# Keeping PSUM copies back to set places, and moving fill transfers to other queues, in a top-k attention and mixture-of-experts kernel

## The chip, the core and the metric

The kernel runs on one core of one Trainium2 chip. A core has TensorE (PE, matmuls; its weight loads are shown as PEld), VectorE (DVE), ScalarE (ACT), GpSimd (POOL) and SyncE (SP). They run side by side, each takes its instructions in the order of its own queue, and semaphores hold an instruction until what it needs is done. Matmuls write to PSUM, and another engine copies the result to SBUF, the working memory. DMA transfers are issued from SyncE's, ScalarE's or GpSimd's queue; 16 DMA engines carry them. The metric is the device time of one execution in microseconds; lower is better.

## The reference

Attention with the 32 largest scores per row, then a mixture of eight experts in which each token goes to the one expert with the largest gate value:

```python
batch, n_heads, seq, head_dim = (8, 8, 576, 64)
scores = scale * np.matmul(q, k.transpose(0, 1, 3, 2))
kth = np.partition(scores, -top_k, axis=-1)[..., -top_k:-top_k + 1]   # top_k = 32
scores = np.where(scores >= kth, scores, -1e9)
attn = softmax(scores); attn_out = np.matmul(attn, v)
x = attn_out.transpose(0, 2, 1, 3).reshape(4608, 512)                 # tokens
logits = x @ w_gate                                                    # 8 experts
e = argmax(logits); gate_w = softmax(logits)[e]
y = gate_w * (np.maximum(x @ w1[e], 0) @ w2[e])      # w1 512x1024, w2 1024x512
```

All of it is in 32-bit floats.

## The kernel before

**Attention.** The work is cut into 160 steps: 8 batches, 4 units of two heads, 5 groups of query tiles (four groups of two tiles of 128 rows, and one group of a single tile). For a step, TensorE forms the scores (`sc`, L244), ScalarE copies them to SBUF (`s`, L253), VectorE folds each row to half its length (`h` and `l`, L260, L262) and finds the threshold of the 32 largest by repeated MAX8 and MATCH_REPLACE8 (L302 to L327). GpSimd scales the threshold (`low`, L329), ScalarE applies it (`depths`, L341), GpSimd subtracts (`less`, L350), ScalarE takes the exponential (`weights`, L361). One step later TensorE transposes the weights (`wTm`, L375, and the rest of the row, `wTl`, L384), ScalarE copies them (`wT`, `wTt`), and at the end of a unit TensorE multiplies with the values (`po`, L405). Scores are formed three steps ahead.

**Routing.** At the end of a batch each token gets its expert and its row in `x_rows`, a buffer in DRAM in which each expert has a stretch of its own. GpSimd scatters the tokens there (L517). After the last batch each expert's last, partly filled block of 128 rows is filled up with blank rows: `fill_up` (L532) waits for all scatters, reads where each expert ends (`value_load`) and issues one transfer of 128 blank rows for each of the eight experts (L539), and one more (L543). In the kernel before, the odd experts' fills are on ScalarE's queue and the even ones' on SyncE's.

**The MoE blocks.** 40 blocks of 128 rows are computed. For each, SyncE loads the rows (`xg`, L612) and the weights of its expert (`w1` and `w2`, 2048 KB each, L604 and L606; two buffers of each, and two of `xg`, whose buffer comes free when the block's result has been stored). `turned` (L622) transposes the rows on TensorE (`xtp`) and copies them out of PSUM (`xTs`, L628). `block` (L630) then does the first layer in two halves of four pieces (`ph`, four matmuls to a piece, L641), each half followed by the ReLU into `hT` on ScalarE (L646), then `py` in eight pieces of one matmul (L650), and the scaled copy `y` (L653). GpSimd stores the rows of `y` (L656). Ahead of `py`, `following` puts out waiting stores and transposes the rows of the next block. `block` is a generator, and each `yield` ends a piece; a block has 16.

**The order.** TensorE, VectorE and ScalarE get their instructions in exactly the order in which the program writes them (`manual_schedule`). `loop` (L850 on) writes one attention step after another, and twice in each step `pieces(n)` runs some pieces of the current block: once between the `wTm` and `wTl` transposes, and once at the end. A rate per batch says how many. So a piece's copies stand on ScalarE at the place where `pieces` happened to reach them. In batches 3 to 8 the loop computes some 24 blocks; two blocks are kept to be run at its end, while the last tokens are routed, and the 14 last ones follow. Four PSUM tiles of MoE work (`xtp`, `ph` twice, `py`) go through two buffers.

The generator's core in the kernel before:

```python
            nc.scalar.activation(hT[:, half * (FT // 2):(half + 1) * (FT // 2), :], ph, AF.Relu)
        following()
        py = k.ps_m.tile([P, Dm], F32, name="py", tag="m")
        for f in range(FT):
            nc.tensor.matmul(py, hT[:, f, :], n.w2[:, 0, f, :], start=(f == 0), stop=(f == FT - 1))
            yield "last" if f == FT - 1 else None
        y = k.mlp.tile([P, Dm], F32, name="y")
        nc.scalar.activation(y, py, AF.Copy, scale=n.x[:, 0, Dm:Dm + 1])
```

Of the kernel before, what the change touches and what calls it, by code (L numbers as in the profile page):

```python
# [11 lines left out]
AF = mybir.ActivationFunctionType  # L12
# [31 lines left out]
def kernel(  # L44
# [487 lines left out]
    def fill_up():  # L532

        ends = k.small.tile([1, E], I32, name="ends")
        nc.vector.tensor_copy(ends, run[0:1, :])
        for e in range(E):
            on = nc.scalar if e % 2 else nc.sync
            r = on.value_load(ends[0:1, e:e + 1], min_val=e * CAP, max_val=e * CAP + N)
            put = on.dma_start(x_rows[bass.ds(r, P), :], blank).ins  # L539
            if not k.exact:  # L540
                for other in scattered:
                    tc.add_manual_dep(put, other.name, WAIT)
        nc.sync.dma_start(x_rows[EMPTY * P:(EMPTY + 1) * P, :], blank)  # L543
# [78 lines left out]
    def turned(n):  # L622

        ps = k.ps_m.tile([P, DT, P], F32, name="xtp", tag="m")
        for dt in range(DT):
            nc.tensor.transpose(ps[:, dt, :], n.x[:, 0, dt * P:(dt + 1) * P], ident)
        n.xT = k.mlp.tile([P, DT, P], F32, name="xTs")
        nc.scalar.copy(n.xT, ps)  # L628

    def block(n, following=lambda: None, put_off=lambda store: store()):  # L630

        if not hasattr(n, "xT"):
            turned(n)
            yield
        hT = k.mlp.tile([P, FT, P], F32, name="hT")
        for half in range(2):
            ph = k.ps_m.tile([P, FT // 2, P], F32, name="ph", tag="m")
            for f in range(FT // 2):
                fc = half * (FT // 2) + f
                for dt in range(DT):  # L640
                    nc.tensor.matmul(  # L641
                        ph[:, f, :], n.w1[:, 0, dt, fc * P:(fc + 1) * P], n.xT[:, dt, :],
                        start=(dt == 0), stop=(dt == DT - 1),
                    )
                yield
            nc.scalar.activation(hT[:, half * (FT // 2):(half + 1) * (FT // 2), :], ph, AF.Relu)  # L646
        following()
        py = k.ps_m.tile([P, Dm], F32, name="py", tag="m")
        for f in range(FT):
            nc.tensor.matmul(py, hT[:, f, :], n.w2[:, 0, f, :], start=(f == 0), stop=(f == FT - 1))  # L650
            yield "last" if f == FT - 1 else None
        y = k.mlp.tile([P, Dm], F32, name="y")
        nc.scalar.activation(y, py, AF.Copy, scale=n.x[:, 0, Dm:Dm + 1])  # L653

        def store():
            put = nc.gpsimd.indirect_dma_start(  # L656
                out=out[:, :], out_offset=bass.IndirectOffsetOnAxis(ap=n.x[:, 0, Dm + 1:XW].bitcast(I32), axis=0),
                in_=y[:, :], in_offset=None, bounds_check=N - 1, oob_is_err=False,
            )
            if not k.exact:  # L660
                tc.add_manual_dep(put.ins, k.last_pool.name, AFTER)

        put_off(store)

    PIECES = 2 * FT
    FIRST = 13
# [5 lines left out]
    with ExitStack() as st:  # L672
# [7 lines left out]
        per_batch = U * len(groups)  # L680
        x_of, lg_of = {}, {}
        waiting, loaded, coming, spare, scatters, stores = [], [], [], [], [], []
        current = ended = None
        left = clock = 0

        def landed(n):
# [5 lines left out]
                loaded[-1].at = clock  # L692

        def put_stores():
            nonlocal current, ended
            while stores:
                stores.pop(0)()
            if ended == "last":
                ended = next(current, "end")
                current = None  # L700

        def following():
            put_stores()
# [1 line left out]
                turned(loaded[0])  # L705

        def pieces(n):
            nonlocal current, left, ended
            if ended == "last":
                ended = next(current, "end")  # L710
                current = None
            while n > 0 and left > 0:
                if current is None:
                    if not landed(loaded[0]):
                        break
                    now = loaded.pop(0)
                    if not hasattr(now, "xT"):
                        turned(now)
                    current = block(now, following, stores.append)
                    ahead()  # L720
                ended = next(current, "end")
                if ended == "end":
                    current = None
                else:
                    n -= 1
                    left -= 1
            return n

        def scatter(n):
# [107 lines left out]
        def loop():  # L837
            nonlocal credit, rate, clock
            for i in range(min(AHEAD, len(work))):
                multiply(i)  # L840
                s_of[i], steps = scores(got_of.pop(i))
                for step in steps:
                    step()
            multiply(AHEAD)
            hl_of[0] = fold(work[0][2], s_of[0])
            for i, (b, u, g) in enumerate(work):
                n = unit[b * U + u]
                if g == groups[0]:
                    open_unit(n)

                if i + 1 < len(work):
                    hl_of[i + 1] = fold(work[i + 1][2], s_of[i + 1])
                low, nbias = search(n, g, s_of[i], *hl_of.pop(i))
                at_place("small")
                w_of[i] = depths(g, s_of[i], low)
                less(g, s_of.pop(i), w_of[i])
                put_stores()
                scatter(1)
                at_place("pool")
                at_place("relu")  # L860
                at = i % per_batch
                if at == FIRST and b:
                    rate = new_of[b - 1] * PIECES / (U * NT)
                credit += rate * len(g)
                room = left
                if b == B - 1 and at >= ARRIVED:
                    room -= KEEP
                    credit = room * len(g) / sum(len(x[2]) for x in work[i:])
                share = 0.5 if g in (groups[0], groups[-2]) else 1.6 if g == groups[2] else 1.2 if g == groups[1] else 1
                now = max(0, min(int(credit * share + 0.5), room))  # L870
                credit -= now
                clock = i
                if i + AHEAD < len(work):
                    s_of[i + AHEAD], steps = scores(got_of.pop(i + AHEAD))
                    for step in steps:
                        step()
                at_place("turn")
                if i:
                    turns = turning(i - 1)
                    next(turns)  # L880
                rest = pieces(now - now // 2)
                if i:
                    next(turns, None)
                weights(n, g, w_of[i], nbias)
                if i + AHEAD + 1 < len(work):
                    multiply(i + AHEAD + 1)
                if g == groups[-2]:
                    end = ending(b, u)
                    late.append([end, next(end)])
                at_place("products")  # L890
                at_place("weights")
                credit = min(credit + pieces(now // 2 + rest), 6 * rate)

            for _ in turning(len(work) - 1):
                pass
            assert len(late) == 1
            clock = None
            for count, _ in enumerate(late[0][0]):
                if count == 4:
                    pieces(6)  # L900
            kept = left - ALWAYS * PIECES
            assert kept == KEEP - 6, kept
            pieces(kept)
# [2 lines left out]
        with tc.manual_schedule(engines={mybir.EngineType.PE, mybir.EngineType.Activation, mybir.EngineType.DVE}):  # L906
            loop()
        pieces(ALWAYS * PIECES)
        put_stores()
        put_stores()  # L910

        any_p = k.small.tile([P, 1], F32, name="any_p")
# [10 lines left out]
    with ExitStack() as outer:  # L923
        either = nc.values_load(rare_i[0:1, 0:1], min_val=0, max_val=P + 1)  # L924
        outer.enter_context(tc.If(either > 0))
        with ExitStack() as st:
            open_pools(st, True)
            more = nc.values_load(rest_i[0:1, 0:1], min_val=0, max_val=LAST)
            with tc.If(more > ALWAYS):
                for slot in spare:  # L930
                    for _ in block(load_block(*slot)):
                        pass
        again = nc.values_load(any_i[0:1, 0:1], min_val=0, max_val=P)
        outer.enter_context(tc.If(again > 0))
        with ExitStack() as st:
# [47 lines left out]
            with tc.For_i(0, NSLOT, 1) as j:  # L983
                now = keep.tile([1, 2], I32, name="now")
                for n in range(2):
                    nc.sync.dma_start(now[:, n:n + 1], slot_d[bass.ds(j + n * NSLOT, 1), :])
                for _ in block(load_block(now[0:1, 0:1], now[0:1, 1:2])):
                    pass


_OUTS = [((4608, 512), 'float32')]
# [40 lines left out]
```

## Time and profile before

| | |
|---|---|
| median of 3 runs | 1626.84 us (1624.94 to 1628.05) |
| profiled execution | 1625.93 us, span 1624.2 us |
| busy: PE, DVE, ACT, POOL | 1348.2, 1263.5, 913.1, 755.1 us |
| granted TensorE clock, mean | 0.906 of full speed |
| moved by DMA | 230.69 MB, 142 GB/s over the span |

The profile is of one execution. Times in it are microseconds from the span's start. Busy time is the time in which an engine executes; a wait is idle time of an engine ahead of an instruction, and it is put down to what ended it (`<-`). "SPq" and "ACTq" are queue entries, such as the issue of a DMA. A line number such as L646 is that of the kernel before; `out<-in` are tile names. "issue" as a releaser means that the engine's own queue was held by instructions that do not count as busy, such as register loads and their waits.

### The profile page before, as it was taken

To read this page: it belongs to the slowest core of one execution; us is meant where nothing else is said; L and a number is where in the kernel's file an instruction comes from. 1 tells how busy PE (TensorE), PEld (TensorE's weight loads), DVE (VectorE), ACT (ScalarE), POOL (GpSimd) and SP (SyncE) were. 2 spreads that over 40 slices of the span, in tenths; PEclk is the share of its full clock that TensorE was granted. 3 is DMA by queue.
4 is the path that set the end of the run, shared out by engine and by line. 5 is a ranking of instruction groups with operands and counts; after the bars stand their busy time and mean duration, and the time that the engine had idled before them with its cause. 6 is when DMAs were issued, how large, how long until landed. Compare 5 with 4: busy or idle time off the path is not lost. (4 is left out here: it accounts for less than half of the span.)

```text
span 1624.2 us, 25229 instructions
## 1 busy us (share of the span) xinstructions
PE 1348.2 (83%) x8034; PEld 891.9 (55%) x8034; DVE 1263.5 (78%) x4130; ACT 913.1 (56%) x1937; POOL 755.1 (46%) x993
## 2 busy tenths in 40 slices
PE   4776677667698989888989988989989995899996
PEld 2443344334465656555656655656656563576764
DVE  7999999999999999999899999999989930000000
ACT  4666666665676667666666766676656640111111
POOL 3555555555555565556544755564546531000000
PEclk9777887886799999999999999999989997899998
DMA  2000011001613343335444443434344638488883
GB/s 60 24 24 23 23 37 40 23 24 36 237 62 143 140 171 136 143 139 170 158 148 180 160 179 140 147 136 167 140 146 154 227 125 291 176 311 307 305 296 132
DMA packets 102191, 230.69 MB, mean 142 GB/s; under 512 B 5150, under 2 KB 25630, under 8 KB 102048
## 3 DMA queue, kind: packets, MB, share of 16 engines
q1 hardware_dynamic: 95328, 209.00, 36.1%
q0 software_dynamic: 6144, 18.92, 3.2%
q8 instruction: 66, 1.08, 0.3%
q10 hardware_dynamic: 576, 1.05, 0.2%
q14 instruction: 77, 0.63, 0.1%
HBM read 207.68 MB, written 22.33 MB: 142 GB/s over the span
## 5 line engine op out<-in xcount | busy, mean ns | idle before, releaser
L350 POOL TENSOR_TENSOR w<-s,w 128x576 f32<-128x576 f32 x288 | 400.3, 1409 | 311.7 <-ACT w L341 311.7
L302 DVE MAX8 tops<-scr 128x8 f32<-128x288 f32 x864 | 361.0, 447 | 3.1
L650 PE MATMUL py<-w,hT 128*128 128x512 f32 x640 | 315.7, 633 | 42.3 <-ACT hT L646 42.3
L641 PE MATMUL ph<-xTs,w 128*128 128x128 f32 x2560 | 322.4, 280 | 25.1 <-ACT xTs L628 25.1
L641 PEld LDWEIGHTS ph<-xTs,w 128*128 128x128 f32 x2560 | 304.5, 194 | 56.3 <-issue 29.8
L341 ACT ACTIVATE w<-s,low 128x576 f32<-128x576 f32 x288 | 209.7, 772 | 101.7 <-POOL low L329 101.3
L244 PE MATMUL sc<-qkb 64*128 64x288 f32 (+1 forms) x1280 | 239.9, 499 | 28.9 <-ACT s L253 23.1
L312 DVE MATCH_REPLACE8 scr<-tops,scr 128x288 f32<-128x288 f32 x576 | 251.0, 441 | 0.0
L361 ACT ACTIVATE w<-w,nbias 128x576 f32<-128x576 f32 x288 | 221.4, 772 | 0.4 <-POOL w L350 0.4
L650 PEld LDWEIGHTS py<-w,hT 128*128 128x128 f32 x640 | 120.0, 201 | 164.4 <-issue 116.3
L329 POOL TENSOR_SCALAR low<-thr 128x2 f32<-128x2 f32 (+1 forms) x160 | 86.3, 540 | 253.1 <-DVE thr L327 246.4
L375 PE MATMUL wTm<-ident,w 128*128 128x128 f32 x1152 | 175.7, 294 | 9.7 <-ACT x L423 8.1
L244 PEld LDWEIGHTS sc<-qkb 64*128 64x128 f32 (+1 forms) x1280 | 123.7, 207 | 97.4 <-ACT s L253 32.3
L375 PEld LDWEIGHTS wTm<-ident,w 128*128 128x128 f32 x1152 | 139.4, 150 | 68.0 <-issue 31.4
L384 PE MATMUL wTl<-ident,w 128*64 128x128 f32 x288 | 66.0, 306 | 131.9 <-ACT wT L378 131.3
L253 ACT COPY s<-sc 128x576 f32<-128x576 f32 x288 | 168.9, 634 | 9.5 <-PE sc L244 9.5
L405 PE MATMUL po<-wT,vb 128*64 128x288 f32 x1024 | 159.8, 461 | 0.6 <-ACT wT L380 0.6
L656 POOL DMA_INDIRECT out_dram<-y,xg x40 | 41.6, 1041 | 251.6 <-ACT y L653 247.8
L378 ACT COPY wT<-wTm 128x512 f32<-128x512 f32 x256 | 139.0, 604 | 3.1 <-PE wTm L375 3.1
L260 DVE TENSOR_TENSOR h<-s 128x576 f32<-128x576 f32 (+1 forms) x160 | 121.0, 756 | 25.0 <-ACT s L253 25.0
L312 DVE MATCH_REPLACE8 scr<-tops,h 128x288 f32<-128x288 f32 x288 | 125.4, 442 | 0.0
L384 PEld LDWEIGHTS wTl<-ident,w 128*64 128x64 f32 x288 | 28.1, 119 | 175.1 <-ACT wT L378 155.1
(124 smaller groups left out, 1491.4 us busy)
## 6 DMA issues: line engine op xcount, KB each, us to landing
w<-in_moe_w_dram SPq DMA_DIRECT2D x80, 2048.0 KB, 12.2
qkb<-in_qk_dram SPq DMA_DIRECT2D x32, 576.0 KB, 3.9
xg<-x_rows SPq DMA_DIRECT2D x40, 257.0 KB, 2.7
vb<-in_v_dram SPq DMA_DIRECT2D x32, 320.0 KB, 3.2
x_rows<-blank SPq DMA_DIRECT2D x5, 257.0 KB, 10.3
x_rows<-blank ACTq DMA_DIRECT2D x4, 257.0 KB, 7.9
x_rows<-x,posi POOLq DMA_INDIRECT x40, 3.1
out_dram<-y,xg POOLq DMA_INDIRECT x40, 2.8
```

Source lines behind the costliest of these rows:

```text
L244: nc.tensor.matmul(ps[rows, j, 0:HF], n.q[d, cols], n.k[d, j * HF:(j + 1) * HF], start=True, stop=True)
L253: lambda m=m, ps=ps: nc.scalar.copy(s[:, m, :, :], ps[:, :, 0:HF]) for m, ps in enumerate(got)
L302: nc.vector.max(out=tops[:, m, r * 8:(r + 1) * 8], in_=src[m])
L312: nc.vector.match_replace(out=scr[:, m, :], in_to_replace=tops[:, m, r * 8:(r + 1) * 8], in_values=src[m], imm_value=NEG,)
L341: nc.scalar.activation(w[:, m, :], s[:, m, :, :].rearrange("p j k -> p (j k)"), AF.Relu, scale=-STEEP, bias=low[:, m:m + 1],)
L350: k.last_pool = in_turn(nc.gpsimd.tensor_tensor(w[:, m, :], s[:, m, :, :].rearrange("p j k -> p (j k)"), w[:, m, :], op=ALU.subtract)).ins
L361: nc.scalar.activation(w[:, m, :], w[:, m, :], AF.Exp, scale=scale, bias=nbias[:, m:m + 1], accum_out=n.z[:, c + m:c + m + 1],)
L375: nc.tensor.transpose(pm[:, c * P:(c + 1) * P], w[:, m, c * P:(c + 1) * P], ident)
L378: nc.scalar.copy(n.wT[:, :, m, tiles[0] * P:(tiles[0] + 1) * P], pm4)
L405: nc.tensor.matmul(po[r, 0:HF], lhsT, rhs, start=(c == 0), stop=(c == KC - 1))
L641: nc.tensor.matmul(ph[:, f, :], n.w1[:, 0, dt, fc * P:(fc + 1) * P], n.xT[:, dt, :], start=(dt == 0), stop=(dt == DT - 1),)
L650: nc.tensor.matmul(py, hT[:, f, :], n.w2[:, 0, f, :], start=(f == 0), stop=(f == FT - 1))
```

## The change

Copies out of PSUM of the MoE blocks are no longer written where `pieces` reaches them. `turned`, the two halves of `block` and its end put them on a list, `due`, and `evacuate` writes out what is on the list, in order. In the loop this is done at two places in each step: behind `depths`, and behind `weights`. Inside `block` it is also done where a PSUM buffer or a result is needed next. After the transposes of the first block, and after the second half of every block, `block` yields "pause": in the loop `pieces` then stops, and goes on at the next of its places, by which time `evacuate` has written the copies. At the end of the program, where `clock` is None, nothing stops at a pause. The copy `y` and its store are put on the list in the same way. The fills of the odd experts go from ScalarE's queue to GpSimd's. The numbers of matmuls, copies and transfers are the same as before.

Where the first block starts, TensorE's rows before (`xtp`: transposed rows of the block, `ph`: its first layer, `wTl`: rest of the weights' transpose, `sc`: next scores, `po`: product with the values):

```order
L375 MATMUL wTm<-ident,w 128x128 x8
L626 MATMUL xtp<-ident,xg 128x128 x4
L641 MATMUL ph<-xTs,w_3831 128x128 x4
L384 MATMUL wTl<-ident,w 64x128 x2
L244 MATMUL sc<-qkb 128x288 x4
L405 MATMUL po<-wT,vb 64x288 x8
```

and now:

```order
L626 MATMUL xtp<-ident,xg 128x128 x4
L384 MATMUL wTl<-ident,w 64x128 x2
L244 MATMUL sc<-qkb 128x288 x4
L405 MATMUL po<-wT,vb 64x288 x8
L405 MATMUL po<-wTt,vb 64x288 x2
L651 MATMUL ph<-xTs,w_3831 128x128 x8
```

The first piece of `ph`, which stood ahead of `wTl`, `sc` and `po`, now stands behind them together with the next.

Late in the loop, ScalarE's rows before (`xTs` and `hT`: the copies of `xtp` and `ph`):

```order
L361 ACTIVATE w,z<-w,nbias 128x576 x2
L407 COPY oT_99<-po 128x288
L646 ACTIVATE hT<-ph 128x512
L628 COPY xTs<-xtp 128x512
L341 ACTIVATE w<-s,low 128x576 x2
L253 COPY s<-sc 128x576
```

and now:

```order
L361 ACTIVATE w,z<-w,nbias 128x576 x2
L656 ACTIVATE hT<-ph 128x512
L407 COPY oT_99<-po 128x288
L341 ACTIVATE w<-s,low 128x576 x2
L628 COPY xTs<-xtp 128x512
L253 COPY s<-sc 128x576
```

`hT` goes directly behind the exponentials, and `xTs` behind the depths (L341); the copy of the scores `s` stays behind `xTs`.

Where the loop ends, the kernel before has on SyncE, behind the load of `w1` for the block after the two kept ones:

```order
L604 DMA w_13697<-in_moe_w_dram 128x4x1024
L538 TENSOR_LOAD ends
L538 ISA x2
L539 ISA
L539 DMA x_rows<-blank 128x514
...
L606 ISA
L606 DMA w_13699<-in_moe_w_dram 128x8x512
...
L543 DMA x_rows<-blank 128x514
```

and on ScalarE:

```order
L784 COPY run<-rank 128x8
L538 TENSOR_LOAD ends
L538 ISA x2
L539 ISA
L539 DMA x_rows<-blank 128x514
...
L646 ACTIVATE hT<-ph 128x512
L628 COPY xTs<-xtp 128x512
```

Of ScalarE's four fills only the first is shown; on SyncE two stand ahead of `w2`, and two and the last one (L543) behind it. Now SyncE has the load of `w2` ahead of all its fills:

```order
L604 DMA w_13697<-in_moe_w_dram 128x4x1024
L606 ISA
L606 DMA w_13699<-in_moe_w_dram 128x8x512
L538 TENSOR_LOAD ends
L538 ISA x2
L539 ISA
L539 DMA x_rows<-blank 128x514
```

and on ScalarE `hT` follows the copy of `run` directly:

```order
L804 COPY run<-rank 128x8
L656 ACTIVATE hT<-ph 128x512
L628 COPY xTs<-xtp 128x512
L680 ACTIVATE y<-py,xg 128x512
L656 ACTIVATE hT<-ph 128x512 x2
```

On GpSimd the four fills stand behind the last five scatters and ahead of the next store of `y`. VectorE's rows are the same in both kernels; GpSimd's and SyncE's differ at this place alone.

The diff, cut to its core:

```diff
@@ fill_up
-            on = nc.scalar if e % 2 else nc.sync
+            on = nc.gpsimd if e % 2 else nc.sync
@@ turned
-        nc.scalar.copy(n.xT, ps)
+        due.append(("xT", lambda: nc.scalar.copy(n.xT, ps)))
+
+    due = []
+
+    def evacuate(upto=None):
+
+        while due and (upto is None or upto in [kind for kind, _ in due]):
+            due.pop(0)[1]()
 
     def block(n, following=lambda: None, put_off=lambda store: store()):
 
         if not hasattr(n, "xT"):
             turned(n)
-            yield
+            yield "pause"
+        evacuate()
         hT = k.mlp.tile([P, FT, P], F32, name="hT")
         for half in range(2):
+            if half:
+                evacuate("y")
             ph = k.ps_m.tile([P, FT // 2, P], F32, name="ph", tag="m")
...
+                if f == FT // 2 - 1:
+                    due.append((f"h{half}", lambda ph=ph, half=half: nc.scalar.activation(
+                        hT[:, half * (FT // 2):(half + 1) * (FT // 2), :], ph, AF.Relu
+                    )))
                 yield
-            nc.scalar.activation(hT[:, half * (FT // 2):(half + 1) * (FT // 2), :], ph, AF.Relu)
+        evacuate("h0")
         following()
+        yield "pause"
+        evacuate()
         py = k.ps_m.tile([P, Dm], F32, name="py", tag="m")
         for f in range(FT):
             nc.tensor.matmul(py, hT[:, f, :], n.w2[:, 0, f, :], start=(f == 0), stop=(f == FT - 1))
-            yield "last" if f == FT - 1 else None
+            if f < FT - 1:
+                yield
         y = k.mlp.tile([P, Dm], F32, name="y")
-        nc.scalar.activation(y, py, AF.Copy, scale=n.x[:, 0, Dm:Dm + 1])
...
+        def scaled():
+            nc.scalar.activation(y, py, AF.Copy, scale=n.x[:, 0, Dm:Dm + 1])
+            put_off(store)
+
+        due.append(("y", scaled))
+        yield "last"
@@ pieces
-                ended = next(current, "end")
-                if ended == "end":
+                if clock is None:
+                    evacuate()
+                step = next(current)
+                if step == "pause":
+                    if clock is not None:
+                        break
+                    continue
+                if step == "last":
                     current = None
-                else:
-                    n -= 1
-                    left -= 1
+                n -= 1
+                left -= 1
@@ loop
                 w_of[i] = depths(g, s_of[i], low)
+                evacuate()
                 less(g, s_of.pop(i), w_of[i])
                 put_stores()
...
                 weights(n, g, w_of[i], nbias)
+                evacuate()
```

More of the change, by code (lines that the diff above doesn't have):

```diff
@@ L661, in store, with whole_block @@
                 tc.add_manual_dep(put.ins, k.last_pool.name, AFTER)
-        put_off(store)
+        def scaled():
[3 more added lines that the diff above has]
+        yield "last"
+    def whole_block(n):
+        for _ in block(n):
+            evacuate()
     PIECES = 2 * FT
@@ L682 @@
         waiting, loaded, coming, spare, scatters, stores = [], [], [], [], [], []
-        current = ended = None
+        current = None
         left = clock = 0
@@ L694, in put_stores @@
         def put_stores():
-            nonlocal current, ended
             while stores:
                 stores.pop(0)()
-            if ended == "last":
-                ended = next(current, "end")
-                current = None
         def following():
@@ L707, in pieces @@
         def pieces(n):
[L708 to L711, printed above, removed]
+            nonlocal current, left
             while n > 0 and left > 0:
@@ L715, in pieces @@
                         break
[L716 to L719, printed above, removed]
+                    current = block(loaded.pop(0), following, stores.append)
                     ahead()
-                ended = next(current, "end")
-                if ended == "end":
+                if clock is None:
[6 more added lines that the diff above has]
+                if step == "last":
                     current = None
-                else:
-                    n -= 1
-                    left -= 1
+                n -= 1
+                left -= 1
             return n
@@ L884, in loop @@
                 weights(n, g, w_of[i], nbias)
+                evacuate()
                 if i + AHEAD + 1 < len(work):
@@ L908 @@
         pieces(ALWAYS * PIECES)
-        put_stores()
+        evacuate()
         put_stores()
@@ L930 @@
                 for slot in spare:
-                    for _ in block(load_block(*slot)):
-                        pass
+                    whole_block(load_block(*slot))
         again = nc.values_load(any_i[0:1, 0:1], min_val=0, max_val=P)
@@ L986 @@
                     nc.sync.dma_start(now[:, n:n + 1], slot_d[bass.ds(j + n * NSLOT, 1), :])
-                for _ in block(load_block(now[0:1, 0:1], now[0:1, 1:2])):
-                    pass
+                whole_block(load_block(now[0:1, 0:1], now[0:1, 1:2]))
 _OUTS = [((4608, 512), 'float32')]
```

## The prediction

> **What bounds the kernel now.** I read the page first, then busy time by stage, then the waits, then the timeline at the places where the change acts. The page gives the span, and VectorE's busy share in 40 slices:
>
> ```profile
> span 1624.2 us, 25229 instructions
> ...
> DVE  7999999999999999999899999999989930000000
> ```
>
> VectorE is busy nine tenths up to slice 32 (about 1313 us) and does nothing later. So there are two stages with different limits: the attention loop, set by VectorE, and what follows it, the "tail", set by TensorE. By stage (columns: stretch, length, busy time with instruction counts of PE, PEld, DVE, ACT and POOL, then granted clock, DMA share, GB/s):
>
> ```profile
> 328.00:1312.00 984.00, 865.20 (x5427) 576.04 (x5427) 944.43 (x3058) 654.20 (x1404) 550.65 (x716) 0.93 0.40 144
> ...
> 1340.00:1367.00 27.00, 9.62 (x39) 6.41 (x39) 3.80 (x25) 1.24 (x3) 4.78 (x5) 0.56 1.00 342
> ...
> 1372.00:1384.00 12.00, 6.19 (x56) 6.00 (x54) 0.00 (x0) 1.20 (x2) 0.99 (x1) 0.96 0.78 262
> ```
>
> While the MoE blocks run in the loop, VectorE is busy 944 of 984 us and TensorE 865. Between them lies the seam, 1340 to 1387: TensorE mostly idle, the DMA engines full. What can come out of the loop is bounded by VectorE's waits there (line, releaser: total, times, longest; the first row is the loop, the second its first 20 us, before any MoE block):
>
> ```profile
> DVE h L260 <- ACT s L253: 25.0, 11, 5.0
> ...
> DVE h L260 <- ACT s L253: 6.6, 2, 5.0
> ...
> PE ph L641 <- ACT xTs L628: 25.1, 6, 5.0
> ...
> PE py L650 <- ACT hT L646: 23.0, 16, 3.1
> ```
>
> 25.0 − 6.6 = 18.4 us in nine waits is the ceiling of the loop's gain. TensorE's two waits, 48 us, are for the copies that the change moves, but TensorE is not what the loop ends on.
>
> The seam, from the timelines of ScalarE, TensorE, SyncE and GpSimd (start, length, what; in brackets the idle time ahead of it):
>
> ```profile
> 1341.07 0.17 ACT L784 COPY run<-rank 128x8 f32<-128x8 f32 x1 [3.65 <-PE rank L486]
> 1357.24 4.08 ACTq L539 DMA_DIRECT2D x_rows<-blank  x4
> 1361.36 0.60 ACT L646 ACTIVATE hT<-ph 128x512 f32<-128x512 f32 x1 [20.13 <-issue]
> ...
> 1340.88 2.77 PE L641 MATMUL ph<-xTs,w 128*128 128x128 f32 x16
> 1362.01 9.03 PE L650 MATMUL py<-w,hT 128*128 128x512 f32 x16 [17.38 <-ACT hT L646]
> 1370.88 7.31 PE L641 MATMUL ph<-xTs,w 128*128 128x128 f32 x64
> 1387.12 1.09 PE L626 MATMUL xtp<-ident,xg 128*128 128x128 f32 x4 [8.93 <-DMA xg<-x_rows]
> 1405.44 7.13 PE L650 MATMUL py<-w,hT 128*128 128x512 f32 x16 [0.25 <-ACT hT L646]
> ...
> 1342.92 0.97 POOL L517 DMA_INDIRECT x_rows<-x,posi  x1 [6.13 <-issue]
> 1348.01 0.91 POOL L517 DMA_INDIRECT x_rows<-x,posi  x1 [0.30 <-issue]
> ...
> 1346.77 0.37 SPq L604 DMA_DIRECT2D w<-in_moe_w_dram  x1
> 1357.12 1.52 SPq L539 DMA_DIRECT2D x_rows<-blank  x2
> 1371.08 0.41 SPq L606 DMA_DIRECT2D w<-in_moe_w_dram  x1
> 1372.25 1.45 SPq L539 DMA_DIRECT2D x_rows<-blank  x2
> 1373.74 0.69 SPq L543 DMA_DIRECT2D x_rows<-blank  x1
> 1384.29 17.60 SPq L612 DMA_DIRECT2D xg<-x_rows  x2
> ```
>
> ScalarE stands from 1341.2 to 1361.4 at four fills, which wait until the last scatters land (1357). Behind them in its queue is the ReLU of a block already computed at 1343.6, call it A; TensorE waits 17.38 us for it. A's late second half then holds the next link: the w2 weights of block C can only load when A's py is done (1371.08), the last three fills stand behind that load on SyncE, C's rows behind the fills, and TensorE waits 8.93 us more for them. SyncE's own waits say the same:
>
> ```profile
> SPq L606 <- PE py L650: 11.6, 1, 11.6
> SPq L539 <- DMA x_rows<-x,posi: 9.0, 2, 8.6
> ```
>
> **The change, part by part. The seam.** ScalarE's four fills go to GpSimd, which has nothing before its next store. A's ReLU then runs at about 1344, and py(A) from 1344.6. It is costed at a cold 9.03 us, so it ends by 1353.6, and B's ph of 7.31 by 1361. Now B's py has xtp(C) ahead of it, and that needs C's rows, so TensorE stops again: the gain is set by when C's rows land, not by the 17.38 us. C's rows need all nine fills. Those need the scatters, 1357 as now. The DMA engines are full, so I count bytes, with the sizes of
>
> ```profile
> w<-in_moe_w_dram SPq DMA_DIRECT2D x80, 2048.0 KB, 12.2
> ...
> x_rows<-blank SPq DMA_DIRECT2D x5, 257.0 KB, 10.3
> ```
>
> From 1340 to 1367 the engines moved 27 × 342 = 9.2 MB: three weight tiles, the scatters and the first six fills. After the change the fourth tile (C's w2, wanted from 1353.6, and in the new order ahead of all SyncE's fills), the three other fills and A's store join that backlog: 2.10 + 0.79 + 0.26 = 3.15 MB, at 342 GB/s 9.2 us more. The last fill lands near 1376.2. Today C's rows reach TensorE 2.83 us after their issue (1387.12 − 1384.29); with 0.3 us to issue, xtp(C) comes at 1379.3 instead of 1387.12: **7.8 us gained**. From there all is as before, py(B) at the cold rate included, since the tail's copies keep their order. Upper bound: the three fills slip in before w2, 0.79 MB or 2.3 us behind 1367, so xtp(C) at 1372.4 and a gain of 14.7. Lower bound: zero. GpSimd's price for a plain DMA is not in the trace; the nearest rows are its scatters, five in 6 us from 1342.92 on, so four fills about 5 us, as on ScalarE (4.08). They end by 1362, far ahead of 1376; only a store of A stands behind them. What is late next is the backlog of bytes.
>
> The Trainium skill, "DMA: Bandwidth & Descriptors" (Issuing engines are not separate DMA queues), says that DMAs from several engines run on the same 16 engines, and that another issuer only saves sequencer time. By that the move would be worth the 4.08 us of issue, and the sum about 1610. The trace disagrees, as 16 of the 20.13 us at this place are a wait that blocks what is queued behind it; on the shared engines it agrees.
>
> **The loop.** Copies of ph, py and xtp move behind set places on ScalarE; none is added, and DVE's, GpSimd's and SyncE's order in the loop stays the same. Three cases of the nine waits:
>
> ```profile
> 765.62 2.08 PE L641 MATMUL ph<-xTs,w 128*128 128x128 f32 x8 [5.04 <-ACT xTs L628]
> 773.92 0.40 ACT L407 COPY oT<-po 128x288 f32<-128x288 f32 x1 [3.87 <-PE po L405]
> 776.09 1.00 DVE L260 TENSOR_TENSOR h<-s 128x576 f32<-128x576 f32 x1 [1.72 <-ACT s L253]
> ...
> 1173.83 0.60 ACT L646 ACTIVATE hT<-ph 128x512 f32<-128x512 f32 x1 [1.89 <-PE ph L641]
> 1185.28 0.58 ACT L628 COPY xTs<-xtp 128x512 f32<-128x512 f32 x1 [4.41 <-PE xtp L626]
> 1184.13 1.11 PE L626 MATMUL xtp<-ident,xg 128*128 128x128 f32 x4 [4.50 <-DMA xg<-x_rows]
> 1188.30 1.71 DVE L260 TENSOR_TENSOR h<-s 128x576 f32<-128x576 f32 x1 [4.48 <-ACT s L253]
> ...
> 799.42 0.69 ACT L653 ACTIVATE y<-py,xg 128x512 f32<-128x512 f32 x1 [1.79 <-PE py L650]
> 802.53 1.70 DVE L260 TENSOR_TENSOR h<-s 128x576 f32<-128x576 f32 x1 [2.30 <-ACT s L253]
> ```
>
> First, TensorE starts a block, waits 5 us for xTs, and wTl, sc and po are queued behind; ScalarE waits for po, and the scores s are late. With the pause, wTl, sc and po go first. Four waits of this kind (1.42, 1.72, 0.62, 1.24) go: 5.0. Second, ReLU hT waits 1.89 us ahead of the depths (L341); so the depths, GpSimd's subtraction and the store behind it are 2.4 us late, then the rows that need the store's buffer, then xTs, with the next depths (1.4 us) behind it. With both copies behind the depths these two waits (4.48, 3.16) lose 3.8 and 3.2: 7.0. Third, y before the depths: behind them it costs s about 1.3 us less, twice: 2.7. Sum 14.7 of the 18.4. I take **10**, two thirds: copies behind the depths now wait for VectorE's threshold, and s stands behind them. Bounds: 18.4, and below nothing, a loss of 8, if none of this comes and new waits of the mean size (18.4 / 9 = 2 us) arise at four block starts.
>
> **The drain** behind the loop has one wait of that second kind, and here TensorE is the limit:
>
> ```profile
> 1313.83 0.63 PE L626 MATMUL xtp<-ident,xg 128*128 128x128 f32 x4 [1.84 <-DMA xg<-x_rows]
> ```
>
> y ahead of the depths made the store and these rows late; it now stands behind: **2 us**, between 0 and 3.
>
> Sum: 10 + 2 + 7.8 = 19.8 us off the profiled execution of 1625.93 us: **1606 us**. That execution is 0.9 us under the median, too little to correct for.
>
> **Rivals.** (1) Only the seam pays: new waits for s take the place of the old. For it: ScalarE is in order, and s still stands behind the moved copies. Against: the new places have weights or depths ahead of them, not behind. 1625.9 − 7.8 = 1618. (2) Only loop and drain pay: C's rows come no sooner, since GpSimd's fills or the w2 load ahead of SyncE's fills hold them. For it: DMA share 1.00; against: idle DMA at 0.78 share from 1372 to 1384. 1614. (3) Both at their tops: 16 in the loop, 2, 14.7: 1593. (4) The loop loses what the seam gains: 1626. (5) Slower: the pause itself. A block's next half may not start until a set place has passed, so TensorE idles once per block and restarts at a low clock. Price: a gap like the 4.50 us at 1184, and 1.9 us for the cold restart (py 9.03 after a gap, 7.13 without), 6.4 us in each of the loop's 24.5 blocks (392 pieces, 16 to a block): 157 us. TensorE has 984 − 865 = 119 us free, so it decides from 4.8 us per block on; then the loop is 38 us longer and the sum 1625.9 − 7.8 + 38 = 1656. Against it: other TensorE work stands in the order behind each pause, and 48 us of waits go.
>
> The Trainium skill, "TensorE: Matmul & The Clock Gate" (HAM oscillation — how this bites in real kernels), warns of idle gaps over some 3.4 us, after which the clock is halved. The 9.03 against 7.13 agrees; by that rule pauses are the risk of case 5.
>
> **How the numbers follow.** Forecast 49%, (1) 18%, (2) 10%, (3) 12%, (4) 5%, (5) 6%. The likeliest case alone spans 1598 to 1613. The range, 1590 to 1622, takes in (1), (2) and (3) and leaves out (4) and (5), 11%. No change means within 0.2% (3.3 us), about what a measurement of this kernel can tell: that is (4), 0.05. Slower 0.06, faster 0.89.
>
> **What would show it.** Right: no idle time of some 20 us ahead of ScalarE's ReLU at the seam, py(A) near 1345 relative to a loop that ends some 10 us earlier, one TensorE gap of about 18 us before xtp(C), that one 7 to 8 us sooner after the scatters than now; VectorE's waits for s between 5 and 10 us after the start; TensorE's waits for xTs and hT in the loop near nothing. Wrong: VectorE's waits as long as before, xtp(C) 30 us behind the last scatter landing as now, or a granted clock in the loop well under 0.93.

## The result, and the profile after

The changed kernel takes **1584.74 us** (median of 4 runs, 1583.78 to 1588.09), the kernel before, timed beside it, 1627.29. The ratio is 0.9745, with a 95% interval of 0.9727 to 0.9763. The prediction was 1606, with a range of 1590 to 1622. So the direction was right, the gain is about twice the predicted one (42 us instead of 21), and the time lies below the range. The profiled execution took 1585.43 us.

The page after, with the two lines that answer to the first ones of the prediction:

```profile
span 1583.8 us, 25232 instructions
...
DVE  7999999999999999999999999999999940000000
```

VectorE is still nine tenths busy to the end of the loop, and does little later. The table cuts both spans at the same three events: VectorE's last threshold (L327), the start of the last rank matmul (L486) and the start of the transposes of block C (`xtp(C)`).

| stretch | before | after | difference | predicted |
|---|---|---|---|---|
| start to last threshold (loop) | 1312.5 | 1283.25 | −29.3 | −10, at most −18.4 |
| last threshold to rank (drain) | 28.2 | 24.4 | −3.7 | −2 |
| rank to xtp(C) (seam) | 46.5 | 41.6 | −4.8 | −7.8 |
| xtp(C) to end (tail) | 237.1 | 234.5 | −2.6 | 0 |
| span | 1624.2 | 1583.8 | −40.4 | −19.8 |

Of the gain the prediction missed, nearly all is in the loop, and the ceiling set for it was broken. Busy time of the engines up to the last threshold shows how (columns as in the prediction's table by stage; the engines are PE, PEld, DVE, ACT, POOL). Before:

```profile
0.00:1312.50 1312.50, 1085.12 (x6568) 705.37 (x6568) 1256.70 (x4094) 863.88 (x1848) 726.86 (x961) 0.90 0.33 116
```

After:

```profile
0.00:1283.25 1283.25, 1083.48 (x6582) 708.32 (x6583) 1239.49 (x4094) 865.94 (x1852) 724.09 (x963) 0.89 0.34 120
```

VectorE executes the same 4094 instructions, and is busy 17.2 us less with them. Its idle time, span less busy, falls from 55.8 to 43.8 us, which is 12.0 less. The 12.0 are the predicted kind of gain, close to the predicted 10; the 17.2 are in no step of the prediction. The waits after:

```profile
DVE h L260 <- ACT s L253: 13.1, 6, 5.2
...
PE py L666 <- ACT hT L656: 3.5, 12, 0.5
```

The wait for s fell from 25.0 us in 11 to 13.1 in 6; TensorE's waits for hT fell from 42.3 us over the whole span to 3.5, and those for xTs (25.1) are gone.

Which of VectorE's instructions became shorter is seen when its groups are split by shape (count, then busy time, mean ns of one, and idle time ahead). Before:

```profile
L260 DVE TENSOR_TENSOR h<-s 128x576 f32<-128x576 f32 x128 | 106.6, 833 | 25.0 <-ACT s L253 25.0
...
L323 DVE TENSOR_TENSOR both<-tops 128x18 f32<-128x18 f32 x128 | 35.8, 280 | 4.2
```

After:

```profile
L260 DVE TENSOR_TENSOR h<-s 128x576 f32<-128x576 f32 x128 | 102.4, 800 | 13.1 <-ACT s L253 13.1
...
L323 DVE TENSOR_TENSOR both<-tops 128x18 f32<-128x18 f32 x128 | 28.5, 222 | 4.2
```

The same 128 folds take 4.2 us less, the same 128 minima of 128x18 take 7.3 less; the small operations for divisors and routing (lines above 400) make up 5.1 more (88.1 to 83.0). The mean hides two kinds of instruction. From VectorE's timeline in the kernel before, a long minimum, a long fold and a fold of the usual length:

```profile
1175.40 1.22 DVE L323 TENSOR_TENSOR both<-tops 128x18 f32<-128x18 f32 x1
...
1188.30 1.71 DVE L260 TENSOR_TENSOR h<-s 128x576 f32<-128x576 f32 x1 [4.48 <-ACT s L253]
1189.93 0.75 DVE L262 TENSOR_TENSOR l<-s 128x576 f32<-128x576 f32 x1
```

GpSimd's timeline there:

```profile
1175.17 2.78 POOL L350 TENSOR_TENSOR w<-s,w 128x576 f32<-128x576 f32 x2 [5.92 <-ACT w L341]
...
1186.62 2.78 POOL L350 TENSOR_TENSOR w<-s,w 128x576 f32<-128x576 f32 x2 [4.36 <-ACT w L341]
```

Each long instruction lies beside GpSimd's subtraction of the depths (1175.17 to 1177.95 and 1186.62 to 1189.40); the fold `l` right behind, with none beside it, takes 0.75. The same minimum (1156.13) and the same long fold (1164.04) in the changed kernel, with the fold that lies between them:

```profile
1156.13 0.18 DVE L323 TENSOR_TENSOR both<-tops 128x18 f32<-128x18 f32 x1
...
1156.50 1.54 DVE L260 TENSOR_TENSOR h<-s 128x576 f32<-128x576 f32 x1
...
1164.04 0.75 DVE L260 TENSOR_TENSOR h<-s 128x576 f32<-128x576 f32 x1
```

No subtraction of depths runs beside any of the three. But the fold between them is long all the same (1.54 us; 1.71 before, at 1176.85). Beside it GpSimd runs another operation:

```profile
1156.15 1.28 POOL L449 TENSOR_TENSOR x<-x,rz 128x640 f32<-128x640 f32 x1
```

In all, 14 of the 128 large folds overlapped a subtraction before and 6 do after; of the minima of 128x18, 17 were longer than 0.23 us before and 10 are after. An estimate from all of VectorE's rows in the loop, which takes the time of each instruction above the usual short value of its group: 68 us before, of which 62 beside a subtraction, and 51 after, of which 40 beside a subtraction. Nearly all the rest lies beside other operations of GpSimd.

The seam after, from TensorE's timeline:

```profile
1310.63 7.13 PE L666 MATMUL py<-w,hT 128*128 128x512 f32 x16
1317.60 7.31 PE L651 MATMUL ph<-xTs,w 128*128 128x128 f32 x64
1349.33 1.09 PE L626 MATMUL xtp<-ident,xg 128*128 128x128 f32 x4 [24.42 <-DMA xg<-x_rows]
```

And from SyncE's (start, time to issue, how many):

```profile
1317.80 0.37 SPq L606 DMA_DIRECT2D w<-in_moe_w_dram  x1
1324.23 12.38 SPq L539 DMA_DIRECT2D x_rows<-blank  x4
1336.65 0.48 SPq L543 DMA_DIRECT2D x_rows<-blank  x1
1346.46 17.58 SPq L612 DMA_DIRECT2D xg<-x_rows  x2
```

The order of events is the predicted one: py(A) runs right after the rank matmuls, B's ph behind it, then one gap until C's rows are there. But xtp(C) comes 41.6 us behind the rank matmul, where the prediction had 38.6, and SyncE's five fills take 13 us to issue.

### The profile page after: what moved, and what is told of

Its sections match the earlier page's. It is cut to its first block, busy times and chain, and to the rows that moved or that the text cites. A ratio compares the mean times of both kernels' runs of the same rounds, so it can differ in the third digit from the quotient of the medians.

```text
span 1583.8 us, 25232 instructions
## 1 busy us (share of the span) xinstructions
PE 1340.4 (85%) x8034; PEld 890.8 (56%) x8034; DVE 1246.2 (79%) x4130; ACT 912.7 (58%) x1937; POOL 753.0 (48%) x997
## 5 line engine op out<-in xcount | busy, mean ns | idle before, releaser
L651 PEld LDWEIGHTS ph<-xTs,w 128*128 128x128 f32 x2560 | 299.7, 192 | 29.3 <-issue 29.2
L651 PE MATMUL ph<-xTs,w 128*128 128x128 f32 x2560 | 316.0, 278 | 0.0
L666 PE MATMUL py<-w,hT 128*128 128x512 f32 x640 | 298.1, 609 | 3.7 <-ACT hT L656 3.5
L341 ACT ACTIVATE w<-s,low 128x576 f32<-128x576 f32 x288 | 209.4, 771 | 100.5 <-POOL low L329 100.3
L375 PEld LDWEIGHTS wTm<-ident,w 128*128 128x128 f32 x1152 | 140.8, 151 | 61.5 <-issue 25.1
L405 PE MATMUL po<-wT,vb 128*64 128x288 f32 x1024 | 164.2, 471 | 0.6 <-ACT wT L380 0.6
L260 DVE TENSOR_TENSOR h<-s 128x576 f32<-128x576 f32 (+1 forms) x160 | 116.8, 730 | 13.1 <-ACT s L253 13.1
L405 PEld LDWEIGHTS po<-wT,vb 128*64 128x64 f32 x1024 | 77.9, 158 | 85.1 <-issue 35.1
```

Source lines behind the costliest of these rows:

```text
L341: nc.scalar.activation(w[:, m, :], s[:, m, :, :].rearrange("p j k -> p (j k)"), AF.Relu, scale=-STEEP, bias=low[:, m:m + 1],)
L375: nc.tensor.transpose(pm[:, c * P:(c + 1) * P], w[:, m, c * P:(c + 1) * P], ident)
L405: nc.tensor.matmul(po[r, 0:HF], lhsT, rhs, start=(c == 0), stop=(c == KC - 1))
L651: nc.tensor.matmul(ph[:, f, :], n.w1[:, 0, dt, fc * P:(fc + 1) * P], n.xT[:, dt, :], start=(dt == 0), stop=(dt == DT - 1),)
```

## The experiments

All ratios are against the kernel before, timed in the same job (1625.5 to 1625.7 us). "A, B, C" are the blocks so named in the prediction.

**Only the fills moved.** The kernel before, with one line of the change:

```diff
-            on = nc.scalar if e % 2 else nc.sync
+            on = nc.gpsimd if e % 2 else nc.sync
```

> The kernel before, with the odd experts' fills on GpSimd's queue and nothing else changed. Theory (the two parts add up; the fills are worth what the profiles show between the last rank matmul and the first transpose of block C, 46.5 against 41.6 us, and some 2 us in the tail): 5 to 8 us faster, about 1620, and VectorE's waits for s stay near 25 us. Rival A (the fills carry the surplus over the forecast, by an earlier start of the last blocks): 15 us faster or more. Rival B (the fills are worth nothing without the earlier drain): within 2 us.

Measured: 1617.96 us, ratio 0.9959 (0.9945 to 0.9972), some 7 us. The loop is as before (last threshold at 1312.5), the seam takes 40.7 us instead of 46.5, and the tail 234.7 instead of 237.1. So the seam's theory holds. The 2.6 us of the tail, which the prediction did not have, cannot be put down to this part of the change: with only the copies moved (next) the tail takes 233.7 us, and in the runs below that leave the tail alone it takes anything from 232.9 to 238.1.

**Only the copies moved.** The changed kernel with that line put back.

> The changed kernel with the odd experts' fills back on ScalarE's queue: copies kept back and pauses alone. Theory: loop and drain are 33 us shorter, as in the profile of the changed kernel (last rank matmul at 1306 against 1339), and the seam is as before: about 1594. Rival A of the fills: no more than 25 us faster.

Measured: 1592.9 us, 0.9795 (0.9771 to 0.9819). The seam takes 47.8 us, and ScalarE's ReLU waits as it did:

```profile
1314.26 0.17 ACT L804 COPY run<-rank 128x8 f32<-128x8 f32 x1 [3.65 <-PE rank L486]
...
1334.49 0.60 ACT L656 ACTIVATE hT<-ph 128x512 f32<-128x512 f32 x1 [20.07 <-issue]
```

The two parts add: 0.9959 × 0.9795 = 0.9755, beside 0.9745 for both. Four fifths of the gain are the copies.

**The pauses taken out.** A block no longer stops at a pause. Where it goes on it writes out itself what is on the list, so the copies of the second half and of the next block's rows are not kept back either; only the first half's ReLU and `y` are:

```diff
                 if step == "pause":
-                    if clock is not None:
-                        break
                     continue
```

> The changed kernel without the pauses: the blocks run on through them, so the copies of the second half and of the next block's transposed rows stand where the pieces reach them, as before; only the first half's ReLU and y are kept back. Theory (the pause does the larger part, as it lets the rest of the weights' transpose, the scores and the values' product go ahead of matmuls that wait): some 20 us slower than the changed kernel, TensorE's waits for xTs and hT in the loop back above 30 us. Rival (the place of the copies alone does it): within 6 us of the changed kernel.

Measured: 1603.96 us, 0.9873 (0.9845 to 0.9901), so 19 us of the gain go. TensorE's waits are back, and VectorE's with them:

```profile
PE ph L651 <- ACT xTs L628: 23.7, 6, 5.0
DVE h L260 <- ACT s L253: 22.1, 11, 5.3
PE py L666 <- ACT hT L656: 21.9, 21, 3.1
```

**The pauses alone.** Blocks pause, but the copies are written right behind the pieces:

```diff
                 n -= 1
                 left -= 1
+            evacuate()
             return n
```

> The changed kernel with the pauses, but the copies written right behind the pieces, ahead of what ScalarE does for the attention next. Theory (a copy ahead of the depths holds up depths, subtraction and scores until TensorE is through): VectorE's waits for s and the folds that run under GpSimd's subtraction come back in part, 8 to 15 us slower than the changed kernel. Rival (the pause alone does it): within 3 us of the changed kernel.

Measured: 1589.38 us, 0.9781 (0.9762 to 0.9801), 5 us more than the changed kernel (the two intervals just touch): between the two expectations. VectorE's wait for s comes back in part, and 12 of the 128 large folds overlap a subtraction:

```profile
DVE h L260 <- ACT s L253: 19.1, 8, 5.2
```

The total hides two opposite terms. Loop and drain are 15.9 us longer than in the changed kernel, but the seam is 8.5 us shorter (33.1 us): here block B's two weight loads were issued 9.3 and 8.3 us ahead of the rank matmul instead of 1.4 and 0.5, so less was probably in the way of C's fills, and SyncE issued four of them in 4.51 us instead of 12.38. By the loop alone, the kernel without pauses ends it at 1301.2 (−11.3) and the pauses without places at 1295.7 (−16.8). Together they make 28.1 of the 29.3, though the first of the two leaves out some of the places as well. The pause, which the prediction had as the one way to be slower, gives more than half of the loop's gain by itself. VectorE's busy time falls in both, to 1249.0 and 1244.6.

**VectorE beside GpSimd, by itself.** A small kernel, which runs 16 folds, 16 minima, 16 MAX8 and 16 MATCH_REPLACE8 on VectorE, first with GpSimd at rest, then beside a row of subtractions.

> A kernel of its own that computes none of the reference: VectorE does 16 folds (128x576 maximum), 16 of the small minimum (128x18), 16 MAX8 and 16 MATCH_REPLACE8, first with GpSimd idle, then all of it again while GpSimd subtracts 128x576 without a pause. Theory (part of the loop's gain is that VectorE's two-operand instructions take longer while GpSimd subtracts): folds 0.75 us alone and 1.4 to 1.7 beside GpSimd, the small minimum 0.18 alone and 0.5 or more, MAX8 and MATCH_REPLACE8 0.45 both times. Rival (the long folds in the kernel have another cause, such as waits that the profile counts as busy): the same durations in both halves.

Measured, first alone, then beside the subtractions (1.26 us each in the mean):

```profile
4.37 12.64 DVE L98 TENSOR_TENSOR h<-s 128x576 f32<-128x576 f32 x16 [2.27 <-DMA s<-in_moe_w_dram]
16.93 3.37 DVE L101 TENSOR_TENSOR both<-tops 128x18 f32<-128x18 f32 x16
20.22 7.89 DVE L104 MAX8 t<-h 128x8 f32<-128x288 f32 x16
...
37.12 25.02 DVE L98 TENSOR_TENSOR h<-s 128x576 f32<-128x576 f32 x16
62.06 10.13 DVE L101 TENSOR_TENSOR both<-tops 128x18 f32<-128x18 f32 x16
72.11 7.89 DVE L104 MAX8 t<-h 128x8 f32<-128x288 f32 x16
```

A fold goes from 0.79 to 1.56 us, a minimum from 0.21 to 0.63, MAX8 stays at 0.49 and MATCH_REPLACE8 at 0.44. So of these four it is the two with two inputs in SBUF that lose, and the search itself (MAX8 and MATCH_REPLACE8, some three quarters of VectorE's busy time) loses nothing.

The Trainium skill, "SBUF — State Buffer" (Who interferes with whom), says just this: VectorE and GpSimd lock a shared pair of ports, a `tensor_tensor` with both inputs in SBUF contends with a GpSimd operation that reads SBUF, and whoever starts second is blocked. The rows above agree as to the contention, and the fold at 1188.30 in the kernel before, which started while a subtraction ran, ended 0.6 us behind the end of that subtraction (1189.40).

**Without the subtraction, before and after.** Both kernels with GpSimd's subtraction left out (its call in the loop, and the scale that goes with it).

> The kernel before without GpSimd's subtraction; so that numbers stay finite, the depths pass the positive scores through, and what is left out is the cut to the 32 largest. Theory: no fold of 128x576 takes over 1 us any more, and VectorE's busy time up to the last threshold is 15 us or more under the 1256.7 us of the kernel before. Rival: long folds and busy time stay.

> The changed kernel without GpSimd's subtraction of the depths; the part left out is that subtraction, so the list of positive candidates is longer, and the thresholds are not the reference's. The kernel before without it took 1562.5 us, with VectorE busy for 1191.0 us up to its last threshold (1256.7 with the subtraction). Theory: the 17 us by which VectorE's own work is shorter in the changed kernel are small operations and folds that no longer fall beside GpSimd's subtractions. Without subtractions there is nothing left to win there: VectorE's busy time up to its last threshold should be within 4 us of 1191.0, and what is left of the change is its seam (5 to 7 us) and waits (12 us) and drain (4 us), so about 1540 us. Rival: the busy time is shorter for another reason (other work of the copies): then it is again 15 us or more below 1191.0, and the time is about 1525 us.

Measured in one run each: 1562.5 us for the kernel before, 1555.1 for the changed one. Up to the last threshold, the kernel before without subtractions:

```profile
0.00:1251.50 1251.50, 1072.73 (x6557) 703.61 (x6558) 1190.97 (x4094) 859.45 (x1843) 332.17 (x677) 0.90 0.35 122
```

The changed kernel without them:

```profile
0.00:1248.90 1248.90, 1073.46 (x6554) 705.64 (x6555) 1191.07 (x4094) 859.76 (x1843) 331.97 (x677) 0.90 0.35 122
```

VectorE's busy time for its 4094 instructions is now the same to 0.1 us. So the whole 17.2 us by which the change shortens VectorE's work exist only where there are subtractions: the theory holds. The kernel before pays 65.7 us for them, the changed one 48.4.

The theory is too narrow in one thing, though: not only operations with two inputs are shorter without subtractions. VectorE's `rz` is the sum of one tile and a constant. In the kernel before, with the subtractions and without:

```profile
L428 DVE TENSOR_SCALAR rz<-z 128x9 f32<-128x9 f32 x32 | 18.2, 570 | 7.0 <-ACT w L361 7.0
...
L428 DVE TENSOR_SCALAR rz<-z 128x9 f32<-128x9 f32 x32 | 5.0, 157 | 13.6 <-ACT w L361 13.6
```

All TENSOR_SCALAR and CAST groups, which have one input tile each, take 40.7 us with the subtractions and 14.3 without: 26 of the 65.7 us. The small kernel had none of them.

The total missed its 1540, though, since the loops differ by only 2.6 us: the 12 us of idle time that the change saves in the full kernels shrink to 2.7 as well (VectorE's wait for s is 27.7 us in the one and 21.2 in the other). Why is open. What is left of the change here is its seam: 46.8 us in the one, 39.9 in the other.

**C's weights later.** Behind the seam, two variants of the changed kernel: the load of C's w2 put behind the load of C's rows on SyncE, or both of its weight loads (the edit of the second is shown).

```diff
-                first = load_weights(SimpleNamespace(), expert)
+                first = SimpleNamespace()
                 fill_up()
                 loaded.append(load_rows(first, piece))
+                late_weights(first, expert)
```

> The changed kernel, with block C's w2 load behind the fills and behind the load of C's rows on SyncE's queue, instead of ahead of them. Theory (the seam ends when C's rows land, and the w2 load ahead of the fills holds SyncE's issue for 8 us and 6 us of transfers): xtp(C) 6 to 11 us sooner after the last rank matmul than the 41.6 us of the changed kernel, about 1576. Rival (the rows wait for the scatters and the fills' own landing, whatever else is queued): within 2 us of the changed kernel.

> The changed kernel, with both weight loads of block C behind the load of C's rows. Theory of the backlog: the scatters too land sooner, since only one block's weights are under way beside them, and xtp(C) comes 12 to 19 us sooner after the last rank matmul than in the changed kernel; C's weights are then late for C's first layer by at most 5 us: 1568 to 1575. Rival (the transfers only change places, and C's first layer waits for w1 as long as C's rows were waited for): no faster than with w2 alone moved.

Measured: 1580.27 us, 0.9719 (0.9694 to 0.9744), with w2 late, and **1577.11 us, 0.9699 (0.9677 to 0.9721)**, with both late; the seam takes 37.9 and 33.0 us instead of 41.6. The second beats both kernels. SyncE's timeline in it:

```profile
1310.46 0.38 SPq L611 DMA_DIRECT2D w<-in_moe_w_dram  x1
1327.15 4.37 SPq L539 DMA_DIRECT2D x_rows<-blank  x4
1331.56 1.33 SPq L543 DMA_DIRECT2D x_rows<-blank  x1
1340.12 0.35 SPq L617 DMA_DIRECT2D xg<-x_rows  x1
1340.72 0.40 SPq L609 DMA_DIRECT2D w<-in_moe_w_dram  x1
1341.36 0.38 SPq L611 DMA_DIRECT2D w<-in_moe_w_dram  x1
```

Four fills are issued in 4.37 us instead of 12.38, so SyncE no longer stands at the first. C's late weights cost nothing at C, since xtp(C), py(B) and ph(C) still follow each other without a gap (1343.04, 1343.92, 1352.52). The tail takes 237.3 us instead of 234.5, however, and TensorE waits for rows there for 6.8 us in seven waits instead of 1.8 in two; whether the late weights put those loads off was not tested. Both gains are under the expected 6 to 11 and 12 to 19 us in the seam, and one thing that the second expectation counted on did not move: the fills still start 17.1 us behind the rank matmul (16.5 in the changed kernel), though C's two loads, issued there 5.4 and 10.1 us behind it, no longer go out before them. What holds the scatters that long was not found.

**Scores first.** The moved copies, the stores and the scatter of a step put behind the copies of scores:

```diff
                 w_of[i] = depths(g, s_of[i], low)
-                evacuate()
                 less(g, s_of.pop(i), w_of[i])
-                put_stores()
-                scatter(1)
...
+                evacuate()
+                put_stores()
+                scatter(1)
```

> The changed kernel with the moved copies of blocks, the stores and the scatter of a step put behind the copies of scores out of PSUM in that step, instead of ahead of them. VectorE still waits 13.1 us in 6 waits for these copies in the changed kernel. Theory: they are late because ScalarE does the moved copies first; with the scores first most of these 13.1 us go, and the time falls by 3 to 8 us, to about 1578 us. Rival: ScalarE's order decides nothing, since the copies of scores are late from TensorE's side or the moved copies then hold TensorE's next matmuls at hT and xTs: the time stays within 3 us of 1584.7, or is longer, with TensorE's waits for hT and xTs (1.3 and 0 us now) back above 5 us.

Measured: 1589.13 us, 0.975 (0.9707 to 0.9794): no gain. VectorE's waits hardly change:

```profile
DVE h L260 <- ACT s L253: 11.4, 5, 5.1
```

The rival holds in its first form: the moved copies on ScalarE are not what makes the remaining scores late. What the loop won (1.6 us) went in the drain, which is 3.2 us longer, and in the tail (3.7 us longer, within the spread of the tails above).

## Why the prediction was wrong, point by point

**The failing step is "25.0 − 6.6 = 18.4 us in nine waits is the ceiling of the loop's gain."** It took VectorE's instructions as of fixed length, without saying so, and only its waits as something to win. But VectorE's busy time holds 65.7 us that are gone when GpSimd's subtractions are left out, and a change of the order alone can move part of them. The loop gave 29.3 us, of which 17.2 come from there. The profile of before showed it: a group whose mean for one form (0.83 us) is well above its common value (0.75), and single folds of 1.7 us in two rows that the prediction itself quotes (1188.30 and 802.53). They were read for their waits alone. A small misreading besides: VectorE does not stop at 1313 us, since the prediction's own row for 1340 to 1367 has it busy for 3.80 us.

How the change moves VectorE's operations off GpSimd's is only partly shown. The pauses and the places each do some of it (1244.6 and 1249.0 against 1256.7). The subtractions come a little sooner behind the threshold (in the mean of the 160 steps a step's first one starts 3.09 us behind the end of the threshold, 3.65 before), so that more of them may be over before VectorE's next minimum; no run moves the subtractions alone. It is not a rule of the order: six of the minima and two of the folds became long in the changed kernel where they had been short.

**The three cases in the loop.** Right in size, and the signs that were named came: 12.0 us of idle time against 10 expected, wait for s from 25.0 to 13.1, TensorE's waits for xTs and hT near nothing. That each wait went for the reason given is not shown one by one, and without the subtractions the same change of order saves only 2.7 us of idle time, which the three cases do not explain. That s still stands behind the moved copies, given as the reason for taking two thirds, cost nothing that "scores first" could win back.

**The drain.** 3.7 us against 2, with bounds of 0 to 3: undersized. The wait of 1.84 us is gone, as forecast. From those transposes to the last rank matmul TensorE takes 26.8 us in both kernels; they start 1.3 us behind VectorE's last threshold before, and 2.3 us ahead of it after. So more came forward than the one wait.

**The seam.** The order of events was right, and so was its reason: the gain is not the 17.38 us of TensorE's wait but when C's rows land. Its size was 4.8 us against 7.8. py(A) was quicker than costed (7.13 us, no cold start), so w2 was issued 10.1 us behind the rank matmul instead of 12.9, and SyncE's issue of the first fill took 8.29 us behind it. With w2 gone from there all four take 4.26 us, and with B's loads earlier 4.51, so the hold goes with how many loads are still under way. The prediction had counted their bytes, but not that the issue of a transfer itself waits. GpSimd's price for four plain transfers, estimated at about 5 us, is 2.32 us:

```profile
1324.86 2.32 POOL L539 DMA_DIRECT2D x_rows<-blank  x4 [8.91 <-DMA x_rows<-x,posi]
```

The prediction's 4.08 us were ScalarE's issue time, all that another issuer saves by the Trainium skill, "DMA: Bandwidth & Descriptors" (Issuing engines are not separate DMA queues). Alone the move is worth 7 us, 5.8 of them in the seam: more than the issue time, as ScalarE no longer stands at the wait ahead of it either.

**The rivals.** Case 3, both at their tops (1593), came nearest, for the wrong reason. Case 5, slower by pauses, is refuted: without pauses the kernel is 19 us slower, and the pauses alone make the loop 16.8 us shorter. From 328 us to the end of the loop TensorE's granted clock is 0.93 before and 0.94 after, so the pauses did not lower it there; other work stands behind each pause, as was held against it. Its chance of 6% was not the fault; that no case was allowed below 1590 was.

## What to carry to other kernels

The waits of the engine that bounds a stage are not always the ceiling of what a change of order can win: split its groups by shape, compare the mean with the common duration, and look at which other engine runs beside the long ones. A wait in an in-order queue is worth what is queued behind it, and behind it stands the next limit; follow the chain one link further than the wait. If a block of work stops to let other engines' work go first, this need not cost anything: here the engine had other work in order behind each pause.

## What the runs showed of the hardware that was not expected

- An operation of VectorE with two inputs in SBUF takes two to three times as long beside GpSimd's subtraction (0.79 to 1.56 us for 128x576, 0.21 to 0.63 for 128x18). In the kernel small operations with one input are longer too (`rz`, 128x9: 0.57 us in the mean, 0.16 without subtractions), and another operation of GpSimd does it as well (a fold of 1.54 us beside L449). Over the loop this is 48 to 66 us.
- The issue of one transfer of 257 KB on SyncE took 8.29 us where four weight loads of 2048 KB had gone out in the 19 us ahead of it (1306.26 to 1317.80). In all five traces with four loads in that time the four issues took 11.0 to 12.5 us together; they took 4.26 us where three had gone out, 4.37 where two had, and 4.51 where two of the four had gone out 8 us earlier.
- The last fill takes 8.6 to 10.5 us from issue to the load that waits for it (1373.74 to 1384.29 before, 1331.56 to 1340.12 with C's weights late), also when the DMA engines are idle a third of that time (share 0.64 from 1333.0 to 1340.1). So it is not the bytes ahead of it alone, as the prediction had it.
